# The second MLP product of nine blocks by seven half-size products in place of eight, with its sums formed on chip

## The chip, the cores and the metric

The kernel runs on one core of one Trainium2 chip. Times are device microseconds (us). Most executions of one kernel agree within some tenths of a per cent; others fall into a slower state, some per cent longer, mostly at a granted TensorE clock below 1. PE is the engine that multiplies, ACT the one for activations and evictions, DVE the vector engine, POOL the GpSimd engine, SP the one that issues transfers. SBUF is the on-chip memory, and a PSUM bank is where a product accumulates.

## The reference

```python
# q, k, v: 4 batches x 8 heads x 768 positions x 64;  4 sinks, window of 128
scores = scale * q @ k.T                    # kept: the first 4 positions and the last 128
a = softmax(where(keep, scores, -1e9))
x = (a @ v)  -> 3072 tokens x 512
h = x @ w_in                                # 512 x 2048
g = h / (1 + exp(-1.702 * h))
out = g @ w_out                             # 2048 x 512
```

Of PE's work the MLP is much the larger part, and it goes block by block: 12 blocks of 256 tokens, each with attention, a first product (64 matmuls of 256 columns) and a second one (32 matmuls of 512 columns).

## The kernel before

The kernel is not written in its final order. Every piece of work is declared with its inputs, a priority and an assumed duration for each engine that may do it. A scheduler then plays all of that through on paper and emits one fixed program for each engine, in the order that it arrived at. In the traces below each engine works off its list in order, and an instruction whose inputs are there waits behind the ones before it: in the changed kernel (e1_again below) DVE starts block 2's first sum at 54.3 us, and POOL's first sum, of the same inputs, starts at 68.13 us, behind weight sums and casts.

```python
class Plan:
    def op(self, eng, dur, lat, fn, deps=(), prio=0.0, acq=None, rel=(), kind=""):
        return self.any({eng: (dur, lat)}, lambda _: fn(), deps, prio, acq, rel, kind)
    ...
        def could(o, e):
            ...
            s = max([free[e], o.begin] + [after(d, e) for d in o.deps])
```

The activation of a block (`gT`, 2048 features x 256 tokens in fp16) comes in eight pieces from DVE, each a tanh from ACT combined with the bank of the first product. The second product takes it as weights:

```python
    def mm2(k):
        ...
        for j, c0, c1 in ((0, 0, 512), (1, 0, 512)) if k < NK - 1 else (...):      # j: half of the tokens
            for s in range(NS):                                                   # NS = 8
                def f(...):
                    for Fi in (2 * s, 2 * s + 1):
                        nc.tensor.matmul(
                            f32(holder[0])[:, 0:w], g[:, Fi, bass.ts(j, P)], w_out16[:, Fi, c0:c1],
                            start=(Fi == 0), stop=(Fi == NF - 1),
                        )
                ...
            # then one eviction by ACT (times 0.5) and two transfers out
```

The softmax here doesn't subtract the row's maximum and nothing guards it: scores larger than these inputs give would overflow.

## Time and profile before

The 222.08 us (median of three; 221.85 to 227.37) divide as follows. Shares are of the profiled execution's span of 220.0 us.

| engine | busy us | share | what it does in the steady part |
|---|---|---|---|
| PE | 213.7 | 97% | both MLP products, scores, attention |
| DVE | 125.9 | 57% | activation pieces, masks, normalising |
| ACT | 125.7 | 57% | tanh, exponentials, evictions |
| POOL | 87.0 | 40% | casts of q, k, v, up to 157 us |

The prediction below shows the page's own lines. The table by stage: for a stretch of time, each engine's busy us with its instruction count in brackets, then granted clock, share of the transfer engines, and GB/s.

```profile
core 0: us, PE busy (x) PEld busy (x) DVE busy (x) ACT busy (x) POOL busy (x), PEclk, DMA share, GB/s
47.00:64.00 17.00, 17.00 (x174) 11.83 (x169) 12.34 (x31) 10.18 (x21) 15.00 (x27) 1.00 0.98 227
64.00:81.00 17.00, 17.00 (x197) 11.84 (x196) 10.50 (x23) 11.75 (x23) 9.27 (x15) 1.00 0.83 195
```

PE is full in both. POOL is nearly full in the first and half free in the second.

### The profile page before, as it was taken

The page shows a single profiled execution, that of the slowest core. Times are in us where ns is not written, and L with a number is a line of the kernel's source. Part 1 is how long each engine was busy: PE and PEld are TensorE (multiplying, and loading weights), DVE is VectorE, ACT ScalarE, POOL GpSimd, SP SyncE. Part 2 cuts the span into 40 slices and gives each one's busy share as a digit, 9 for nine tenths or more (in the row PEclk, how much of TensorE's full clock was granted, in tenths as well). Part 3 has the DMA queues.
Part 4 walks back from the last instruction along what each step waited for, and adds up shares of the span by engine and source line. Part 5 has one row for each costly group of instructions (what it writes and reads, how often), then busy time and mean ns, then how long its engine had stood idle before and what let it go on. Part 6 is the DMA issues. An engine that isn't in the chain of part 4 may idle for free.

```text
span 220.0 us, 5209 instructions
## 1 busy us (share of the span) xinstructions
PE 213.7 (97%) x2066; PEld 143.8 (65%) x2066; DVE 125.9 (57%) x274; ACT 125.7 (57%) x243; POOL 87.0 (40%) x150
## 2 busy tenths in 40 slices
PE   7889999999999999999999999999999999999993
PEld 3448777577757766666666667657667666666642
DVE  2678855397826855656556664666465655634310
ACT  2597645777557576475485476466466486444320
POOL 2596431689971956704905727508500000000000
PEclk9999999999999999999999999999999999999998
DMA  5999999999979589289498589398541312231223
GB/s 162 355 236 204 207 302 202 324 302 289 210 141 240 143 182 295 51 166 297 103 205 240 73 204 250 84 213 232 106 91 47 71 27 48 52 68 26 51 48 95
DMA packets 65911, 36.54 MB, mean 166 GB/s; under 512 B 27968, under 2 KB 61120, under 8 KB 65888
## 3 DMA queue, kind: packets, MB, share of 16 engines
q1 hardware_dynamic: 60848, 30.19, 56.0%
q0 software_dynamic: 4592, 5.37, 12.9%
q10 hardware_dynamic: 448, 0.66, 1.1%
q8 instruction: 16, 0.26, 0.5%
q14 instruction: 7, 0.06, 0.1%
HBM read 27.56 MB, written 6.29 MB: 154 GB/s over the span
## 4 chain that ended last, share of the span: by engine, by line
PE 91%; DMA 4%; ACT 2%; SPq 1%; issue 0%; DVE 0%
PE bank L736 39%; PE bank L765 37%; PE bank L669 6%; PE bank L604 5%; DMA qk<-in_q_dram 3%; PE bank L532 1%; DMA out_dram<-osb 1%; ACT at L629 1%; ACT v L286 1%; PE bank L596 1%; PE bank L584 1%; PE bank L708 1%; SPq L407 0%; PE bank L846 0%; ACT blkT L286 0%
## 5 line engine op out<-in xcount | busy, mean ns | idle before, releaser
L765 PE MATMUL bank<-w_out,gT 128*128 128x512 f16 (+2 forms) x400 | 99.8, 371 | 0.0
L736 PE MATMUL bank<-xT,w_in 128*128 128x256 f16 x768 | 99.8, 273 | 0.0
L750 DVE SCALAR_TENSOR_TENSOR gT<-th,bank 128x512 f16<-128x512 f16 x96 | 65.5, 683 | 48.8 <-ACT th L748 47.8
L748 ACT ACTIVATE th<-bank 128x512 f16<-128x512 f32 x96 | 57.7, 603 | 62.0 <-PE bank L736 61.3
L736 PEld LDWEIGHTS <-w_in 128*128 128x128 f16 x768 | 72.9, 98 | 23.8 <-issue 1.7
L286 POOL CAST qk<-qk 64x512 f16<-64x512 f32 (+1 forms) x74 | 44.9, 609 | 45.1 <-DMA qk<-in_q_dram 41.9
L629 ACT ACTIVATE at<-bank 128x512 f16<-128x512 f32 (+1 forms) x96 | 48.7, 569 | 10.9 <-PE bank L604 10.9
L765 PEld LDWEIGHTS <-gT 128*128 128x128 f16 x400 | 36.1, 98 | 23.3 <-issue 1.4
L636 DVE TENSOR_TENSOR at<-at,bank 128x1024 f16<-128x1024 f16 (+1 forms) x40 | 25.7, 643 | 22.8 <-ACT at L629 22.8
L286 POOL CAST v<-v 64x512 f16<-64x512 f32 (+1 forms) x43 | 26.1, 606 | 8.9 <-DMA v<-in_v_dram 6.8
L669 PE MATMUL bank<-v,at 128*128 128x65 f16 x352 | 21.2, 193 | 0.1
L784 ACT ACTIVATE osb<-bank 128x512 f32<-128x512 f32 (+1 forms) x24 | 14.4, 600 | 11.0 <-PE bank L765 11.0
L669 PEld LDWEIGHTS <-at 128*128 128x128 f16 x352 | 17.5, 97 | 4.2 <-DVE at L636 0.3
L689 DVE TENSOR_TENSOR xb<-bank,rcp 128x256 f16<-128x256 f32 x36 | 15.2, 422 | 0.7
L669 PE MATMUL bank<-vs,ats 128*128 128x65 f16 x128 | 14.7, 193 | 0.0
L604 PEld LDWEIGHTS <-blkT 64*128 64x128 f16 x256 | 8.0, 94 | 9.3 <-issue 7.8
L604 PE MATMUL bank<-blkT 64*128 64x256 f16 x192 | 13.4, 244 | 0.0
L669 PEld LDWEIGHTS <-ats 128*128 128x128 f16 x128 | 12.0, 97 | 2.0
L687 DVE RECIPROCAL rcp<-bank 128x4 f32<-128x4 f32 x48 | 8.4, 177 | 3.6 <-PE bank L669 3.2
L286 ACT COPY blkT<-bank 128x256 f16<-128x256 f16 (+1 forms) x12 | 5.1, 463 | 4.4 <-PE bank L532 4.3
L604 PE MATMUL bank<-blkT,blkT 64*128 64x128 f16 x64 | 7.2, 222 | 0.0
L846 PE MATMUL bank<-zero 128*128 128x512 f16 x19 | 5.8, 463 | 1.2 <-DVE zero L304 1.2
(43 smaller groups left out, 68.4 us busy)
## 6 DMA issues: line engine op xcount, KB each, us to landing
v<-in_v_dram SPq DMA_DIRECT2D x12, 512.0 KB, 6.7
out_dram<-osb SPq DMA_DIRECT2D x46, 128.0 KB, 2.4
qk<-in_q_dram SPq DMA_DIRECT2D x8, 512.0 KB, 5.3
qk<-in_k_dram SPq DMA_DIRECT2D x8, 512.0 KB, 6.7
w_in<-in_moe_w_in_dram POOLq DMA_DIRECT2D x4, 512.0 KB, 9.5
w_out<-in_moe_w_out_dram POOLq DMA_DIRECT2D x4, 512.0 KB, 12.8
qk<-in_q_dram SPq DMA_DIRECT2D x6, 256.0 KB, 5.3
qk<-in_k_dram SPq DMA_DIRECT2D x4, 256.0 KB, 5.5
```

Source lines behind the costliest of these rows:

```text
L286: {"POOL": nc.gpsimd.tensor_copy, "DVE": nc.vector.tensor_copy, "ACT": nc.scalar.copy}[e](out=out, in_=in_)
L604: nc.tensor.matmul(f32(o_s, 2 * n + i)[:, c : c + w], src[d, j], Q[d].rearrange("d j s -> d (j s)")[:, q0 : q0 + w], start=k >= KM, stop=T ...
L629: nc.scalar.activation(out=A[:, i, 0:W], in_=f32(o_s, 2 * n + i)[:, 0:W], func=AF.Exp, scale=scale)
L636: nc.vector.tensor_tensor(out=A[:, :, 0:W], in0=A[:, :, 0:W], in1=mask(c0, c0 + W).unsqueeze(1).to_broadcast((P, 2, W)), op=ALU.mult,)
L669: nc.tensor.matmul(avp()[:, j, i], a_, v_, start=(n == 0), stop=(n == len(mms) - 1))
L687: o_r = op("DVE", 93, 190, lambda: nc.vector.reciprocal(out=rc, in_=avp()[:, :, :, D]), [o_a], prio=base - 1.2 * h8, kind="rcp")
L689: o_n = op("DVE", 340, 430, lambda: nc.vector.tensor_tensor(out=X, in0=avp()[:, :, :, 0:D], in1=rc.to_broadcast((P, 2, 2, D)), op=ALU.mult ...
L736: nc.tensor.matmul(f32(holder[0])[:, bass.ts(e, TB)], w_in16[:, c, bass.ts(Fi, P)], X[:, c] if k < KX else X2[:, :, c], start=(c == 0), st ...
L748: o_t = op("ACT", 477, 600, lambda first=first: nc.scalar.activation(out=th[first.places[0]], in_=f32(first), func=AF.Tanh, scale=0.851), ...
L750: o_g[k, s] = op("DVE", 590, 700, lambda first=first, s=s: nc.vector.scalar_tensor_tensor(out=g[:, 2 * s : 2 * s + 2].rearrange("p a t -> ...
L765: nc.tensor.matmul(f32(holder[0])[:, 0:w], g[:, Fi, bass.ts(j, P)], w_out16[:, Fi, c0:c1], start=(Fi == 0), stop=(Fi == NF - 1),)
L784: nc.scalar.mul(O[:, c0:c1], f32(holder[0])[:, 0:w], 0.5)
```

## The change

Strassen's scheme multiplies two 2x2 matrices of blocks with seven block products instead of eight, at the price of sums of blocks on both inputs and of the results. Here the blocks are halves of the tokens and of the feature pairs on the one side, halves of the features and of the output columns on the other. PE loses an eighth of the second product's columns in blocks 2 to 10; POOL and DVE get the sums. The core of the diff:

```diff
-    RS, RQ, RV, RA, RX, RG, RTH, RO = 3, 2, 4, 6, 3, 5, 3, 3
+    RS, RQ, RV, RA, RX, RG, RTH, RO = 3, 2, 4, 4, 3, globals().get('OPT',{}).get('RG',3), 3, 2
+    KS, LASTS = globals().get('OPT',{}).get('KS',2), globals().get('OPT',{}).get('LASTS',NK-1)
...   # the third input buffer is a tile "third", whose room three of the weight sums take over later
+    def forms_of_w():                       # once: 4 x 5 sums of 128 x 512 fp16
+        for j in range(4):
+            for n, (a, b_, what) in enumerate((((0, 0), (1, 1), ALU.add), ...)):
+                def f(eng, j=j, n=n, a=a, b_=b_, what=what):
+                    x = slice(2 * j, 2 * j + 2)
+                    (nc.gpsimd if eng == "POOL" else nc.vector).tensor_tensor(
+                        out=wf[n][:, x], in0=W[:, x, a[0], a[1]], in1=W[:, x, b_[0], b_[1]], op=what)
+                ...
+                o_wf[j, n] = plan.any({"POOL": (OPT_("WFP", 800), OPT_("WFP", 800) + 100), **({"DVE": (350, 450)} if OPT_("WFD", 0) else {})}, ...)
+    def forms_of_g(k):                      # each block: 4 x (DVE sum, DVE difference, POOL sum)
+        for s in range(0, NS, 2):
+            def f1(x=x):
+                nc.vector.tensor_tensor(out=F[:, x, 0:2], in0=G[:, x, 0:2], in1=G[:, x, 2:4], op=ALU.add)
+            def f2(x=x):
+                nc.vector.tensor_tensor(out=G[:, x, 1:3], in0=G[:, x, 1:3], in1=G[:, x, 0::3], op=ALU.subtract)
+            def f3(eng, x=x):
+                (nc.gpsimd if eng == "POOL" else nc.vector).tensor_tensor(
+                    out=F[:, x, 2], in0=G[:, x, 0], in1=G[:, x, 3], op=ALU.add)
+    def mm2_by_seven(k):                    # 56 matmuls of 256 columns, in three banks
+        last = run(2, lambda s: [(0, G[:, s, 0], wf[1][:, s]), (1, G[:, s, 3], wf[2][:, s])], hu, ...)
+        ...   # ACT: lone = .5 half;  DVE: lone += .5 other half
+        last = run(4, lambda s: [(0, F[:, s, 2], wf[0][:, s])], hy, ...)
+        ...   # DVE: lone += .5 of it
+        last = run(2, lambda s: [(0, F[:, s, 0], W[:, s, 1, 1]), (1, F[:, s, 1], W[:, s, 0, 0])], hu, ...)
+        ...   # ACT evicts two quarters; POOL: part = lone - them (fp32)
+        last = run(2, lambda s: [(0, G[:, s, 2], wf[4][:, s]), (1, G[:, s, 1], wf[3][:, s])], hw, ...)
+        ...   # DVE: the other two quarters = .5 of the bank + part; four transfers out
+    def second(k):
+        if KS <= k < LASTS:
+            mm2_by_seven(k)
+        else:
+            mm2(k)
```

In the views, `third` and `wf` are the weight sums, `gF` and the second writing of `gT` the activation sums, and L863 the new matmuls.

More of the change, by code (lines that the diff above doesn't have):

```diff
@@ L253 @@
     vs32 = pool.tile([P, B, E], FP32, name="vs32")
-    qk32 = ring("qk32", RS, (P, 2, H, 2, D), FP32)
-    v32 = ring("v32", RS, (P, H, 2, D), FP32)
+    third = pool.tile([P, 3 * H * 2 * D], FP32, name="third")
+    qk32 = ring("qk32", RS - 1, (P, 2, H, 2, D), FP32)
+    v32 = ring("v32", RS - 1, (P, H, 2, D), FP32)
+    qk32.append(third[:, 0 : 2 * H * 2 * D].rearrange("p (e h i d) -> p e h i d", e=2, h=H, i=2))
+    v32.append(third[:, 2 * H * 2 * D :].rearrange("p (h i d) -> p h i d", h=H, i=2))
+    wf = [third[:, 1024 * n : 1024 * n + 1024].bitcast(FP16).rearrange("p (s c) -> p s c", s=NS) for n in range(3)]
+    wf += ring("wf", 2, (P, NS, d_model // 2), FP16)
+    gF = ring("gF", 2, (P, NS, 3, P), FP16)
+    part = pool.tile([P, 512], FP32, name="part")
+    lone = pool.tile([P, 256], FP32, name="lone")
     qk16 = ring("qk16", RQ, (P, 2, 2, H, D), FP16)
@@ L265 @@
     gT = ring("gT", RG, (P, NF, TB), FP16)
-    osb = ring("osb", RO, (P, d_model), FP32)
+    osb = ring("osb", RO, (P, 2 * d_model), FP32)
     bank = [psp.tile([P, 512], FP32, name=f"bank{i}") for i in range(8)]
-    plan = Plan(8, {"m": 1, "s": 5, "t": 4, "a": 2, "x": 2, "h": RTH, "o": 2})
+    OPT_ = globals().get("OPT", {}).get
+    plan = Plan(8, {"m": 1, "s": 5, "t": 4, "a": 2, "x": 2, "h": RTH, "o": OPT_("NO", 3)})
     op = plan.op
@@ L394, in load @@
         b, r = divmod(k, R)
-        sl = k % RS
+        sl = k if k < RS else (k - 1) % (RS - 1)
         t0 = r * TB
@@ L719 @@
     o_g = {}
-    n_o = [0]
     def mm1(k):
@@ L775, in mm2 @@
             if not c0:
-                oi = n_o[0] % RO
-                n_o[0] += 1
-                war = reuse("osb", oi)
-            O = osb[oi]
+                war = reuse("osb", (k % RO, j))
+            O = osb[k % RO][:, bass.ts(j, d_model)]
             row = k * TB + j * P
@@ L798, in mm2 @@
                 o_d = op(eng, 590, (420, 4), f, o_c, prio=prio, kind="out")
-                uses("osb", oi, o_d)
+                uses("osb", (k % RO, j), o_d)
+    def forms_of_w():
+        W = w_out16.rearrange("p (s e) (h c) -> p s e h c", e=2, h=2)
+        for j in range(4):
+            for n, (a, b_, what) in enumerate((((0, 0), (1, 1), ALU.add), ((0, 1), (1, 1), ALU.subtract), ((1, 0), (0, 0), ALU.subtract),
+                                    ((0, 0), (0, 1), ALU.add), ((1, 0), (1, 1), ALU.add))):
+                def f(eng, j=j, n=n, a=a, b_=b_, what=what):
+                    x = slice(2 * j, 2 * j + 2)
+                    (nc.gpsimd if eng == "POOL" else nc.vector).tensor_tensor(
+                        out=wf[n][:, x], in0=W[:, x, a[0], a[1]], in1=W[:, x, b_[0], b_[1]], op=what)
+                free = []
+                if n < 3:
+                    free = [o for (kk, _, _), o in o_cqk.items() if kk == 2] + [o for p in range(NP) for o in o_cv[2, p]]
+                o_wf[j, n] = plan.any({"POOL": (OPT_("WFP", 800), OPT_("WFP", 800) + 100), **({"DVE": (350, 450)} if OPT_("WFD", 0) else {})},
+                                      f, [o_w[4 + j]] + free, prio=nominal(KS + 1, -9 + j), kind="wf")
@@ new lines, in forms_of_g @@
+    def forms_of_g(k):
+        g, F = gT[k % RG], gF[k % 2]
+        G = g.rearrange("p (s e) (t q) -> p s (e t) q", e=2, t=2)
+        war = reuse("gF", k % 2)
+        for s in range(0, NS, 2):
+            x = slice(s, s + 2)
+            def f1(x=x):
[5 more added lines that the diff above has]
+                    out=F[:, x, 2], in0=G[:, x, 0], in1=G[:, x, 3], op=ALU.add)
+            prio = nominal(k, s + OPT_("GF", 3)) + 3
+            deps = [o_g[k, s], o_g[k, s + 1]]
+            a = op("DVE", 335, 440, f1, deps + war, prio=prio, kind="gf")
+            b_ = op("DVE", 335, 440, f2, deps + [a], prio=prio, kind="gf")
+            e3 = OPT_("F3", "POOL").split()
+            c = plan.any({e: {"POOL": (450, 550), "DVE": (200, 300)}[e] for e in e3}, f3, deps + war, prio=prio, kind="gf")
+            for i in (s, s + 1):
+                o_f[k, i] = (a, b_, c)
@@ new lines, in mm2_by_seven, with run, f, at @@
+    def mm2_by_seven(k):
+        g, F, O, T = gT[k % RG], gF[k % 2], osb[k % RO], part
+        G = g.rearrange("p (s e) (t q) -> p s (e t) q", e=2, t=2)
+        W = w_out16.rearrange("p (s e) (h c) -> p s e h c", e=2, h=2)
+        N = d_model // 2
+        u = [0]
+        def run(n_s, what, first, deps, fresh, acq=None):
+            prev = None
+            holder = first
+            for s0 in range(0, NS, n_s):
+                def f(s0=s0):
+                    for s in range(s0, s0 + n_s):
+                        for half, lhs, rhs in what(s):
+                            nc.tensor.matmul(f32(holder[0])[:, bass.ts(half, N)], lhs, rhs, start=fresh and s == 0 and half == 0,
+                                             stop=s == NS - 1, skip_group_check=True)
+                n = n_s * len(what(0))
+                o = op("PE", n * pe_ns(N), (n - 1) * pe_ns(N) + N / 2.4 + 166, f,
+                       deps(range(s0, s0 + n_s)) + ([prev] if prev else []), prio=at(),
+                       acq=None if holder else acq, kind="mm2")
+                u[0] += 1
+                if not holder:
+                    holder.append(o)
+                uses("gT", k % RG, o)
+                uses("gF", k % 2, o)
+                prev = o
+            return prev
+        def at():
+            return nominal(k + 1, 8 * u[0] / 14) + 3
+        def fw(n, S):
+            return [o_wf[s // 2, n] for s in S]
+        hu, hy, hw = [], [], []
+        last = run(2, lambda s: [(0, G[:, s, 0], wf[1][:, s]), (1, G[:, s, 3], wf[2][:, s])], hu,
+                   lambda S: [o_g[k, s] for s in S] + fw(1, S) + fw(2, S), True, ("o", 1))
+        o_x = op("ACT", 263, 390, lambda: nc.scalar.mul(lone, f32(hu[0])[:, 0:N], 0.5), [last] + reuse("lone", 0), prio=at(), kind="y")
+        o_y = op("DVE", 335, 440, lambda: nc.vector.scalar_tensor_tensor(
+            out=lone, in0=f32(hu[0])[:, N : 2 * N], scalar=0.5, in1=lone, op0=ALU.mult, op1=ALU.add), [o_x], prio=at(), kind="y")
+        last = run(4, lambda s: [(0, F[:, s, 2], wf[0][:, s])], hy,
+                   lambda S: [o_f[k, s][2] for s in S] + fw(0, S), True, ("o", 1))
+        o_z = op("DVE", 335, 440, lambda: nc.vector.scalar_tensor_tensor(
+            out=lone, in0=f32(hy[0])[:, 0:N], scalar=0.5, in1=lone, op0=ALU.mult, op1=ALU.add), [last, o_y], prio=at(), rel=[(hy[0], 0)], kind="y")
+        last = run(2, lambda s: [(0, F[:, s, 0], W[:, s, 1, 1]), (1, F[:, s, 1], W[:, s, 0, 0])], hu,
+                   lambda S: [o_x, o_y] + [o_f[k, s][0] for s in S], False)
+        war = reuse("osb", (k % RO, 0)) + reuse("osb", (k % RO, 1))
+        o_u = op("ACT", 477, 600, lambda: nc.scalar.mul(O[:, N : 3 * N], f32(hu[0]), 0.5), [last] + war,
+                 prio=at(), rel=[(hu[0], 0)], kind="oc")
+        o_t = plan.any({e: {"POOL": (1100, 1200), "DVE": (600, 700)}[e] for e in OPT_("TE", "POOL").split()},
+            lambda eng: (nc.gpsimd if eng == "POOL" else nc.vector).tensor_tensor(
+            out=T.rearrange("p (n c) -> p n c", n=2), in0=lone.unsqueeze(1).to_broadcast((P, 2, N)),
+            in1=O[:, N : 3 * N].rearrange("p (n c) -> p n c", n=2), op=ALU.subtract),
+            [o_z, o_u] + reuse("part", 0), prio=at(), kind="t")
+        uses("lone", 0, o_t)
+        last = run(2, lambda s: [(0, G[:, s, 2], wf[4][:, s]), (1, G[:, s, 1], wf[3][:, s])], hw,
+                   lambda S: [o_f[k, s][1] for s in S] + fw(3, S) + fw(4, S), True, ("o", 1))
+        o_v = op("DVE", 600, 700, lambda: nc.vector.scalar_tensor_tensor(
+            out=O.rearrange("p (n c) -> p n c", n=4)[:, 0::3], in0=f32(hw[0]).rearrange("p (n c) -> p n c", n=2), scalar=0.5,
+            in1=T.rearrange("p (n c) -> p n c", n=2), op0=ALU.mult, op1=ALU.add),
+            [last, o_t], prio=nominal(k + 1, 8) + 3, rel=[(hw[0], 0)], kind="oc")
+        uses("part", 0, o_v)
+        for j in range(2):
+            row = k * TB + j * P
+            for i in range(2):
+                def f(i=i, j=j, row=row):
+                    nc.sync.dma_start(
+                        out[row : row + P].rearrange("(p i) f -> i p f", i=2)[i], O[64 * i : 64 * i + 64, bass.ts(j, d_model)])
+                o_d = op("SP", 590, (420, 4), f, [o_v, o_u], prio=nominal(k + 1, 8) + 4, kind="out")
+                uses("osb", (k % RO, j), o_d)
@@ L801 @@
+    o_wf, o_f = {}, {}
+    def second(k):
[3 more added lines that the diff above has]
+            mm2(k)
     for j_ in range(8):
@@ L811 @@
             mm1(k_ - 1)
+            if KS <= k_ - 1 < LASTS:
+                forms_of_g(k_ - 1)
+        if k_ == 2:
+            forms_of_w()
         if k_ >= 2:
-            mm2(k_ - 2)
+            second(k_ - 2)
     mm1(NK - 1)
-    mm2(NK - 2)
-    mm2(NK - 1)
+    if LASTS == NK:
+        forms_of_g(NK - 1)
+    second(NK - 2)
+    second(NK - 1)
     loads += o_vl + [o_more]
```

## The prediction

> **What bounds the kernel now.** I read the page's part 1 first, then the slices, the chain that ended last, the groups by form, and last the timeline. Part 1 and three rows of the slices:
>
> ```profile
> span 220.0 us, 5209 instructions
> PE 213.7 (97%) x2066; PEld 143.8 (65%) x2066; DVE 125.9 (57%) x274; ACT 125.7 (57%) x243; POOL 87.0 (40%) x150
> ...
> PE   7889999999999999999999999999999999999993
> DVE  2678855397826855656556664666465655634310
> POOL 2596431689971956704905727508500000000000
> PEclk9999999999999999999999999999999999999998
> ```
>
> PE is at 9 from slice 4 to the last but one, at full clock; DVE and ACT are near half. POOL matters though it shows 40%: it has nothing after slice 31 and is at 9 in slices 9 to 10, 13 and 19. Is the busy PE really streaming? The chain, merged in time, shows the spacing (start, us, what):
>
> ```profile
> PE 91%; DMA 4%; ACT 2%; SPq 1%; issue 0%; DVE 0%
> ...
> 206.12 0.87 PE bank L736 x8
> 208.73 4.33 PE bank L765 x20
> 214.22 2.37 DMA out_dram<-osb
> ```
>
> Eight 256-column products (first MLP product) take 0.87 us, 109 ns each; twenty 512-column ones (second) 4.33 us, 216 ns each: a column costs the same in either shape. From 20 us on the table by stage gives PE 10.00 of 10.00 and 17.00 of 17.00 in each stretch up to 200 us, so a column taken away there shortens the time, if the rest keeps up. The list of waits has PE waiting three times, 2.6 us in all, before 15 us. The bound is the number of columns through PE.
>
> The groups that I size with (busy us, mean ns | idle before):
>
> ```profile
> L736 PEld LDWEIGHTS <-w_in 128*128 128x128 f16 x768 | 72.9, 98 | 23.8 <-issue 1.7
> L750 DVE SCALAR_TENSOR_TENSOR gT<-th,bank 128x512 f16<-128x512 f16 x96 | 65.5, 683 | 48.8 <-ACT th L748 47.8
> L636 DVE TENSOR_TENSOR at<-at,bank 128x1024 f16<-128x1024 f16 x28 | 19.2, 685 | 16.9 <-ACT at L629 16.9
> L689 DVE TENSOR_TENSOR xb<-bank,rcp 128x256 f16<-128x256 f32 x36 | 15.2, 422 | 0.7
> L479 POOL TENSOR_TENSOR vs<-vs,more 128x520 f16<-128x520 f32 x4 | 4.2, 1054 | 0.3
> L784 ACT ACTIVATE osb<-bank 128x512 f32<-128x512 f32 x23 | 13.9, 604 | 9.0 <-PE bank L765 9.0
> ```
>
> [...] The mask product (L636) agrees: 546 ns at 768 elements and 685 at 1024 is 0.54 ns an element. [...] No DVE instruction of the steady part before has two SBUF inputs (each one's second input is PSUM)[...]; the change adds eight per block. [...] L479 gives 1054/520 = 2.0 ns, on fp32 inputs; no 16-bit two-input sum on POOL is in the trace.
>
> **The change part by part.**
>
> *PE.* A block's second product is 2 x 16 matmuls of 512 columns: 32 x 215.8 ns = 6.91 us. By seven products it is 7 x 8 of 256 columns: 56 x 109.2 = 6.12 us. Saved 0.79 us a block, times 9 blocks: **7.1 us**. I counted the built programs too: 400 matmuls become 112 + 504, and the sum of PE's work at these spacings falls from 204.0 to 196.8 us, nothing else altered. There are 216 more weight loads of 98 ns, but the first MLP product loads 128 columns of weights per 256-column matmul already and still runs at 109, so they stay hidden.
>
> *ACT.* Two evictions of 604 ns become one of 604 and one of 128x256 (388 by the L616 group of that form): 0.2 us a block less. Nothing.
>
> *DVE, per block.* Four sums and four differences of 512 fp16 elements, 685 - 512 x 0.54 = 407 ns each: 3.26 us; two combinations of 256 out of PSUM, 422 each (form of L689): 0.84; one of 512, 683: 0.68. Together 4.8 us recorded, some 4 net, since consecutive DVE records overlap by about 0.09 (99.12 to 99.71 us for a 0.66 record). A 17 us stretch holds 9.4 to 12.3 us now; a block of about 16 us would then hold 13 to 14.5: **some 85%**. It still fits.
>
> *POOL, per block.* Twelve casts at 0.65 spacing (8 in 5.29 us): 7.8; four sums of 256, at 2 ns about 0.55: 2.2; one fp32 of 512: 1.05. That is 11 of 16 us, fine in the long run.
>
> *POOL, once.* Twenty weight sums of 512, between 0.8 us (what the kernel's scheduler assumes) and 1.05 (L479): 16 to 21 us, all before block 2's second product. This is where I expect loss. Before, POOL between 40 and 65 us is packed:
>
> ```profile
> 40.39 2.62 POOL L286 CAST v<-v 64x512 f16<-64x512 f32 x4 [6.79 <-DMA v<-in_v_dram]
> 43.07 2.28 POOL L286 CAST qk<-qk 128x512 f16<-128x512 f32 x4
> 45.30 2.61 POOL L286 CAST v<-v 64x512 f16<-64x512 f32 x4
> ...
> 49.10 5.29 POOL L286 CAST qk<-qk 64x512 f16<-64x512 f32 x8
> 54.45 2.59 POOL L286 CAST v<-v 64x512 f16<-64x512 f32 x4
> 57.11 5.18 POOL L286 CAST qk<-qk 64x512 f16<-64x512 f32 x8
> ```
>
> In the new order eight weight sums lie ahead of the casts of block 2's v, in the idle time there; twelve come after 43 us. I add up in the built order, with the shorter and the longer size: casts of block 4's q and k end at 60.9 (62.9) instead of 54.4; of block 5's at 72.6 (75.5) instead of 62.3; the last of block 2's POOL sums at 73.0 (76.0). PE's program places the first scores of block 4 at 62.2 us of its work, the last use of that sum at 62.7, the first scores of block 5 at 69.4. Before, time runs 8.2 us ahead of that work (64.24 us at 56.07 of work). Casts to landed transpose is 6.5 us (tile blkT's landing). So block 4's scores are safe (67.4 or 69.4 against 70.4 plus), the last sum is late by 1.5 us (about 4.5), and block 5's scores then lose little more. [...] I take **2.2 us**. Four weight sums also come before block 2's q and k casts at 31.07; these then end about 2 us later, while PE's transposes of them were moved back 0.9 us: **0.6 us**.
>
> *Steady part.* [...] The bank of a first-product group has room (three in turn, a group every 2 us, tanh plus product 1.3), so most is hidden; I take **0.1 us a block, 0.9 us**.
>
> *Rings and end.* gT 5 to 3, input buffers 3 to 2, at 6 to 4 copies: each still allows about a block of lead. The last block stays in the old form, so the end (PE alone, then 2.4 us of output) stays.
>
> Sum: 222.1 - 7.1 + 2.2 + 0.6 + 0.9 = **218.7 us**; I set 218.4, as orders like this one are usually shaped until they run well.
>
> **Rivals.** *A: PE takes it all.* For: PE waits for nothing now, the other engines average 57% and less. Then 215 us. *B: DVE becomes the bound* [...] With 0.6 us a block lost: 221 us or more. *C: POOL in one stage only* (my choice): the loss comes once, between 60 and 85 us, and later blocks run at 0.79 us less each. *D: weight loads bound the 256-column matmuls*, the gain vanishes at 222; against it stands L736 at 109 ns.
>
> **Range and chances.** A gives the low end, 215.2; B with C the high end, 222.0. Faster by 2% needs under 217.6, which is stage losses of 2.7 us or less in place of my 3.7: 0.40. Within 2%: 0.55. Slower by 2%, over 226.5, needs DVE or POOL as a full bound: 0.05.
>
> **What would show it.** PE: 504 matmuls of 128x256 in the new line at 109 ns spacing, PE work down by 7 us; another spacing is D. POOL: weight sums between 0.8 and 1.05 us; slices 6 to 13 at 9; PE's list of waits with POOL sums or a transposed qk as releasers near 70 to 80 us, 1.5 to 4.5 us in all. Port: the DVE sums over 407 ns in the mean, above all where POOL is busy, near 407 after its casts end. Stretches of 17 us after 100 us with PE full prove A or C there; PE idle in each of them proves B. I am wrong if PE is full throughout (faster than said), or if DVE is at 9 in most slices (slower).

The sum came to 222.1 - 7.1 + 2.2 + 0.6 + 0.9 = 218.7 us and was set to 218.4. The 0.9 us (steady part), a share of the 2.2 us (POOL, once) and rival B rested on a passage by which DVE and POOL hold each other up, the author's estimate, not shown at the time ("Port" in its last paragraph is the name for it). 109.2 ns is the mean of 491 spacings of L736 in the trace of the kernel before, and 215.8 ns that of its longest run of L765 at 512 columns (14 matmuls; all 217 spacings average 216.2 ns). The mask product's 0.54 ns an element is measured, with one input in PSUM.

## More of the kernel before

The casts of q, k and v from fp32 to fp16 fall mostly to POOL, in time that nothing else wants:

```python
        ns = {"POOL": (n / 0.96 + 30, n / 0.96 + 130), "DVE": (n / 1.92 + 65, n / 1.92 + 165),
              ...
```

## The result, and the profile after

The changed kernel is correct and took 225.77 us (median of four, 225.32 to 230.92), against 222.15 for the kernel before beside it (median of four, 221.85 to 227.37). The ratio is 1.016, with a 95% interval of 1.013 to 1.020. Ratios here are the mean time of one kernel's fast runs over that of the other's fast runs of the same rounds, so they are not quite the ratio of the medians. By the 2% rule that counts as the same; it is surely not faster, and it lies above the predicted range.

The first profile of the changed kernel fell into the slow state (clock 0.985), so the lines below are from its repetition `e1_again`, at full clock, 225.42 us. The page, parts 1 and 2:

```profile
span 223.6 us, 5862 instructions
...
PE 209.5 (94%) x2282; PEld 164.8 (74%) x2282; DVE 176.4 (79%) x372; ACT 123.1 (55%) x244; POOL 152.1 (68%) x215
...
PE   7989999999794689999999999999999999999993
...
POOL 2596498899999999999659998599696232131200
```

A digit is 5.6 us. PE has a dent in the eleventh (56 to 61 us) and a hole from the thirteenth to the fifteenth (67 to 84 us), and looks full elsewhere. POOL stands at 8 or 9 from the sixth to the nineteenth (28 to 106 us). The chain that ended last, by engine, was 91% PE before; now a quarter of it is POOL:

```profile
PE 45%; POOL 26%; DVE 16%; issue 4%; ACT 4%; DMA 3%; SPq 1%; DVEq 0%; POOLq 0%; ACTq 0%
```

The same two stretches as before, by stage:

```profile
47.00:64.00 17.00, 15.84 (x165) 11.17 (x162) 15.76 (x36) 9.46 (x20) 16.39 (x21) 1.00 0.67 185
64.00:81.00 17.00, 11.20 (x131) 8.83 (x130) 11.20 (x17) 7.25 (x15) 16.20 (x24) 1.00 0.33 66
```

PE now idles 1.16 and 5.80 us of these, 7.0 us in all; POOL is full in both. From 81 to 183 us PE idles another 1.7 us. Outside these stretches its idle time is what it was, less 0.8 us at the start. The list of PE's waits (what it waited for: us in total, times, longest) names POOL first and DVE second, and the timeline of PE shows the two long ones (start, us, what, and in brackets the idle time before it):

```profile
PE bank L863 <- POOL gF L836: 5.0, 2, 2.6
PE bank L679 <- DVE at L646: 2.1, 4, 1.2
```

```profile
72.26 0.39 PE L863 MATMUL bank<-third,gF 128*128 128x256 f16 x2 [2.46 <-POOL gF L836]
...
78.95 0.39 PE L863 MATMUL bank<-third,gF 128*128 128x256 f16 x2 [2.58 <-POOL gF L836]
```

These are block 2's second product, waiting for activation sums on POOL. The timeline of POOL says what it was doing instead:

```profile
49.53 9.31 POOL L816 TENSOR_TENSOR third<-w_out 128x512 f16<-128x512 f16 x8
58.77 5.57 POOL L296 CAST qk<-qk 64x512 f16<-64x512 f32 x8
64.43 3.74 POOL L816 TENSOR_TENSOR third<-w_out 128x512 f16<-128x512 f16 x3
...
72.78 5.37 POOL L296 CAST qk<-qk 64x512 f16<-64x512 f32 x8
78.23 1.29 POOL L836 TENSOR_TENSOR gF<-gT 128x256 f16<-128x256 f16 x2
```

Weight sums, casts, sums, casts, in the order that the scheduler had fixed. Of the block's four sums the second and third stand behind the casts of v (from 68.74 us) and start at 71.48 us; the fourth stands behind eight casts of q and k. The fourth ends near 78.9 us, the first of the last line's two.

The DVE wait is a second mechanism. Timeline of DVE, then of PE, from the same execution:

```profile
55.45 1.26 DVE L834 TENSOR_TENSOR gT<-gT 128x512 f16<-128x512 f16 x1
56.63 0.54 DVE L646 TENSOR_TENSOR at<-at,bank 128x768 f16<-128x768 f16 x1
```

```profile
57.23 0.35 PE L679 MATMUL bank<-v,at 128*128 128x65 f16 x6 [1.16 <-DVE at L646]
```

The DVE difference of 512 elements, sized at 0.41 us, took 1.26 us, while POOL was in its run of weight sums of 1.16 us each; the mask product queued behind it, and PE waited 1.16 us for that. The groups by form (busy us, mean ns | idle before) show that this is the rule and not one case:

```profile
L836 POOL TENSOR_TENSOR gF<-gT 128x256 f16<-128x256 f16 x36 | 26.4, 734 | 27.0 <-DVE gT L759 24.2 <-PE bank L614 1.8
L834 DVE TENSOR_TENSOR gT<-gT 128x512 f16<-128x512 f16 x36 | 24.9, 693 | 0.8
...
L832 DVE TENSOR_TENSOR gF<-gT 128x512 f16<-128x512 f16 x36 | 23.1, 640 | 0.7
...
L816 POOL TENSOR_TENSOR third<-w_out 128x512 f16<-128x512 f16 x12 | 14.2, 1214 | 0.2
```

The DVE differences average 693 ns and the DVE sums (L832) 640 ns. The timeline also shows what they take alone: the two at 187.68 and 188.13 us overlap no POOL instruction and took 0.41 and 0.42 us. In the first profile seven of the 72 overlap none, and these took 408 to 425 ns, against means of 660 and 705 ns. So two inputs in SBUF are not slow in themselves. The eight weight sums of the other group (`wf`) took 1153 ns each.

So there are two suspects: the twenty weight sums on POOL before block 2 (called W), and DVE and POOL holding each other up (called P). The texts, the labels and the code call P "the port". That is a name here: the runs show how much the two engines' instructions lengthen beside each other, and not what they share.

### The profile page after: what moved, and what is told of

It is laid out like the page before. It is cut to its first block, busy times and chain, and to the rows that moved or that the text cites. A ratio compares the mean times of both kernels' runs of the same rounds, so it can differ in the third digit from the quotient of the medians.

```text
span 229.1 us, 5862 instructions
## 1 busy us (share of the span) xinstructions
PE 211.8 (92%) x2282; PEld 166.2 (73%) x2282; DVE 178.0 (78%) x372; ACT 123.3 (54%) x244; POOL 151.5 (66%) x215
## 4 chain that ended last, share of the span: by engine, by line
PE 51%; POOL 20%; DVE 12%; issue 3%; DMA 2%; ACT 1%; DVEq 0%; POOLq 0%; ACTq 0%
PE bank L745 22%; PE bank L863 13%; POOL qk L296 8%; PE bank L774 7%; POOL third L816 6%; PE bank L679 5%; DVE gT L759 4%; POOL gF L836 2%; POOL v L296 2%; PE bank L614 2%; DVE gT L834 2%; DMA xT<-xb 2%; DVE at L646 2%; DVE gF L832 1%; POOL part L899 1%
## 5 line engine op out<-in xcount | busy, mean ns | idle before, releaser
L836 POOL TENSOR_TENSOR gF<-gT 128x256 f16<-128x256 f16 x36 | 26.6, 740 | 27.6 <-DVE gT L759 26.0
L863 PEld LDWEIGHTS <-gT 128*128 128x128 f16 x288 | 27.1, 98 | 5.5 <-DVE gT L759 1.4
L834 DVE TENSOR_TENSOR gT<-gT 128x512 f16<-128x512 f16 x36 | 25.4, 705 | 0.8
L863 PEld LDWEIGHTS <-gF 128*128 128x128 f16 x216 | 20.1, 98 | 7.9 <-POOL gF L836 5.6
L832 DVE TENSOR_TENSOR gF<-gT 128x512 f16<-128x512 f16 x36 | 23.8, 660 | 0.7
L774 PE MATMUL bank<-w_out,gT 128*128 128x512 f16 (+2 forms) x112 | 23.9, 349 | 0.0
L863 PE MATMUL bank<-w_out,gF 128*128 128x256 f16 x144 | 21.0, 273 | 0.0
L899 POOL TENSOR_TENSOR part<-lone,osb 128x512 f32<-128x512 f32 x9 | 11.5, 1280 | 13.0 <-ACT osb L896 12.7
L863 PE MATMUL bank<-wf,gT 128*128 128x256 f16 x144 | 20.0, 273 | 0.0
L863 PE MATMUL bank<-third,gT 128*128 128x256 f16 x144 | 19.0, 273 | 0.9 <-POOL third L816 0.8
```

Source lines behind the costliest of these rows:

```text
L774: nc.tensor.matmul(f32(holder[0])[:, 0:w], g[:, Fi, bass.ts(j, P)], w_out16[:, Fi, c0:c1], start=(Fi == 0), stop=(Fi == NF - 1),)
L832: nc.vector.tensor_tensor(out=F[:, x, 0:2], in0=G[:, x, 0:2], in1=G[:, x, 2:4], op=ALU.add)
L834: nc.vector.tensor_tensor(out=G[:, x, 1:3], in0=G[:, x, 1:3], in1=G[:, x, 0::3], op=ALU.subtract)
L836: (nc.gpsimd if eng == "POOL" else nc.vector).tensor_tensor(out=F[:, x, 2], in0=G[:, x, 0], in1=G[:, x, 3], op=ALU.add)
L863: nc.tensor.matmul(f32(holder[0])[:, bass.ts(half, N)], lhs, rhs, start=fresh and s == 0 and half == 0, stop=s == NS - 1, skip_group_check ...
```

## The experiments

Each was built from the changed kernel. Before is the kernel before in the same job, with fast runs of 221.3 to 222.4 us wherever a ratio is given. "Wrong" means that the output is not right and only the time counts. A few of the fast runs had a granted clock of about 0.99 (226.10 of e1_again, 223.37 of e12); with the runs nearer full clock alone, e1_again would be 1.016 and e12 0.996, which changes no reading below.

| run | what it is | fast runs, us | ratio to before (95%) |
|---|---|---|---|
| e1_again | the change as it is | 225.42, 226.10 | 1.018 (1.014 to 1.021) |
| e2_noport | DVE sums read PSUM for one input; wrong | 222.00, 222.43 | 1.002 (0.999 to 1.005) |
| e3_nowsum | weight sums of 4 columns; wrong | 218.95, 220.42 | 0.990 (0.985 to 0.996) |
| e4_neither | both | 216.81 to 218.87 | 0.981 (0.975 to 0.986) |
| e5_rings | the smaller buffer rings alone, old product | 221.48 to 221.88 | 1.000 (0.998 to 1.001) |
| e6_late4 | seven products from block 4 on | 218.51 to 219.30 | 0.987 (0.984 to 0.989) |
| e7_late4_known | the same, better informed scheduler | 216.16 to 217.39 | 0.976 (0.973 to 0.979) |
| e8_late3_dve | from block 3 on, weight sums on DVE or POOL, informed | 215.24 to 216.87 | 0.973 (0.970 to 0.977) |
| e12_sizes_again | e6 with measured durations only | 220.32 to 223.37 | 1.000 (0.992 to 1.008) |
| e13_noport_again | e6 with DVE sums reading PSUM; wrong | 215.96 to 216.88 | 0.976 (0.973 to 0.978) |
| e14_neither_again | e4, ordered with measured durations; wrong | 214.68 to 215.94 | 0.971 (0.968 to 0.975) |
| e15_late3_again | e8's kernel again | 215.29 to 216.47 | 0.973 (0.970 to 0.977) |

### The change again, and each suspect taken away (one job)

**e1_again** is the changed kernel unchanged, for a clean profile and a reference on this chip.

> The changed kernel itself once more, for a profile in the fast state (the first fell in the slow one) and as the yardstick of the other three. All theories: about 225.5 us, ratio to before 1.015. PE should wait some 5 to 8 us between 45 and 100 us, on POOL's weight sums and on the block-2 activation sums of POOL, as in the first profile.

It came as before, 1.018.

**e2_noport** takes P away without altering any order or dependency: the second input of each DVE activation sum becomes a constant that lies in PSUM.

```diff
-                nc.vector.tensor_tensor(out=F[:, x, 0:2], in0=G[:, x, 0:2], in1=G[:, x, 2:4], op=ALU.add)
+                nc.vector.tensor_tensor(out=F[:, x, 0:2], in0=G[:, x, 0:2], in1=mask(0, 512).rearrange("p (a b c) -> p a b c", a=2, b=2), op=ALU.add)
...   # f2 likewise
```

> Wrong result on purpose. The order of all engines is kept; the eight DVE sums of a block take their second input from a PSUM tile (the mask) in place of SBUF, 16-bit and of the same size. Theory P[...]: DVE sums fall from about 680 ns to about 410, POOL weight sums and casts shorten too where a DVE sum had blocked them, time falls by 2 to 4 us to about 222. Theory W (POOL's own weight sums in one stage are the loss[...]): time falls by under 1.5 us. Rival S (the sums are slow by their shape[...]): they stay near 680 ns and the time stays.

```profile
L836 POOL TENSOR_TENSOR gF<-gT 128x256 f16<-128x256 f16 x36 | 24.0, 669 | 28.7 <-DVE gT L759 22.3 <-PE bank L614 4.6 <-DVE rcp L697 0.8
...
L834 DVE TENSOR_TENSOR gT<-gT,bank 128x512 f16<-128x512 f16 x36 | 15.0, 416 | 0.8
```

The same instruction, in the same place of the same program, went from 693 to 416 ns; L832 from 640 to 415. POOL gained too: its sums from 734 to 669 ns, its casts of q and k from 664 to 609, so the blocking goes both ways. Rival S of the expectation, slow by shape, falls. The time fell by 1.018 - 1.002, 1.6% or 3.5 us of 221.8, and the two intervals do not touch. PE became full from 47 to 64 us, but from 64 to 81 us it still idled 5.2 us: P is real and does not explain the hole.

**e3_nowsum** takes W away in the same manner: each weight sum keeps its place and its dependencies but handles 4 columns in all.

```diff
-                        out=wf[n][:, x], in0=W[:, x, a[0], a[1]], in1=W[:, x, b_[0], b_[1]], op=what)
+                        out=wf[n][:, x, 0:2], in0=W[:, x, a[0], a[1], 0:2], in1=W[:, x, b_[0], b_[1], 0:2], op=what)
...   # the matmuls read quarters of w_out in place of the sums: same shapes, same count
```

> Wrong result on purpose. Order kept; each of the twenty weight sums on POOL is cut to 2 columns of its 256 and the matmuls read quarters of the weight itself in their place, so no matmul waits for a weight sum and POOL is some 20 us freer between 28 and 75 us. Theory W: PE's idle time between 45 and 100 us goes from 6 or 7 us to under 2 and the time falls by 5 us or more, to 220 or less. Theory P: it falls by 2 to 3 us, the rest of the loss is spread over all blocks.

PE's waits for POOL are gone from its list, and the stretch of the hole reads:

```profile
64.00:81.00 17.00, 16.07 (x203) 13.30 (x201) 14.59 (x30) 9.74 (x20) 11.91 (x17) 1.00 0.67 154
```

PE idles 0.93 us there instead of 5.80. The time fell by 1.018 - 0.990, 2.7% or 6.1 us. W is the larger cause.

**e4_neither** does both edits.

> Wrong result on purpose: both edits of the two runs before it. If port and weight sums are the whole loss, PE keeps its saving of 7 us and the time is 215 to 216 us. If rings, DVE's plain load or the order cost something as well, it stays above 217.

The ratio is 0.981, 8.2 us below the change. The two single effects add up to 9.6 us. An overlap is plausible, as some of P's blocking happens behind weight sums: in e3 the DVE sums fell to 617 and 651 ns. But 1.4 us is no more than the intervals allow. Fully hidden sums would have left 0.968 (7.1 us below 221.8), so about 2.8 us were still unaccounted for.

### Buffers, and a later start (another job)

**e5_rings** keeps the old product everywhere and takes over only the smaller rings and the shared tile.

```diff
+OPT = {'KS': 12}
...
-        if k_ == 2:
-            forms_of_w()
```

> Correct result. The changed kernel with no block by seven products and no weight sums: what is left of the change is its smaller buffers (two input buffers after block 2, three gT, four at, two double-width osb). Theory R (the smaller rings cost time): 223 us or more. Theories W and P: as before, 222 us within 0.5.

1.000 within 0.2%: with the old product the smaller buffers cost nothing. With the new one they were not varied; e14 below, which keeps them, leaves about 0.7 us for them and all else.

**e6_late4** asks whether W is a matter of when. One number moves the start of the new product from block 2 to block 4, which gives up two of the nine savings (1.6 us). All twenty weight sums remain, of full size, on POOL.

```diff
+OPT = {'KS': 4}
```

> Correct result, one number changed: seven products in blocks 4 to 10 in place of 2 to 10, which lets the scheduler put the weight sums some 35 us later. The saving on PE is 7 x 0.79 = 5.5 us in place of 7.1. Theory W: the stage loss of about 6 us goes almost wholly, the port's loss stays: 222.0 - 5.5 + 2 to 3 = 219 us. If the weight sums hurt wherever they stand: 222 us or more.

0.987, and correct. The stretch of the hole, and POOL in it:

```profile
64.00:81.00 17.00, 17.00 (x197) 11.76 (x196) 10.36 (x23) 11.55 (x23) 16.54 (x20) 1.00 0.71 171
```

```profile
66.11 11.17 POOL L817 TENSOR_TENSOR third<-w_out 128x512 f16<-128x512 f16 x10
```

POOL now does ten weight sums in a row at 66.11 us, 11.17 us long, in a stretch where before it was half free, and PE is full, 17.00 of 17.00, in each of the three stretches from 47 to 98 us. The sums take 1152 ns each, as before: their cost is their deadline and not their amount. What remains is 1.56 us of PE idle time from 115 to 132 us, behind DVE.

**e7_late4_known** tells the scheduler what the traces showed: POOL's durations as measured, and a rule that keeps DVE's two-input sums and POOL's work apart, since they lengthen beside each other (640 and 693 ns in e1_again, 415 and 416 in e2).

```diff
+        port = [0.0]
+        def on_port(o, e):
+            return o.kind in (("cqk", "cv", "ks", "vs", "gf", "wf", "t") if e == "POOL" else ("gf", "wf")) and e in ("POOL", "DVE")
...
+            if on_port(o, e):
+                s = max(s, port[0])
...
+            if on_port(o, e):
+                port[0] = s + dur - 20
...   # POOL: cast n / 0.96 + 30 -> + 117;  weight sum 800 -> 1165;  activation sum 450 -> 675;  fp32 sum 1100 -> 1280
```

> Correct result. As the run before it, but the kernel's scheduler is given the measured durations (POOL weight sum 1.165 us for 0.8, POOL activation sum 0.675 for 0.45, fp32 sum 1.28 for 1.1, cast 0.65 for 0.56) and keeps two-input DVE sums and POOL work from overlapping. No instruction is added or removed. If the rest of the loss is an order made for wrong sizes and a port it did not know, this is faster than the run before it by 1 to 2 us: 217 to 218 us. If the port's waits themselves bind DVE, it is not.

0.976: another 1.0% off, with no arithmetic altered. The DVE sums (L832 and L834's counterparts) fell from 728 and 628 ns in e6 to 572 and 474; the first of the two, in e6 and then in e7:

```profile
L833 DVE TENSOR_TENSOR gF<-gT 128x512 f16<-128x512 f16 x28 | 20.4, 728 | 0.6
...
L841 DVE TENSOR_TENSOR gF<-gT 128x512 f16<-128x512 f16 x28 | 15.9, 572 | 0.3
```

**e8_late3_dve** starts one block earlier and lets the scheduler place weight sums on DVE.

```diff
+OPT = {'KS': 3, 'WFD': 1}
...   # and the scheduler of e7
```

> Correct result. The informed scheduler, seven products in blocks 3 to 10, and weight sums on either DVE or POOL as the scheduler finds room. Saving on PE 8 x 0.79 = 6.3 us; with little loss 216 to 217 us, the best so far, and faster than the kernel before by over 2%. If DVE, near 85% busy, can't take the eight or more microseconds of weight sums too, 219 us or more.

It put 18 of the 20 weight sums on DVE, at 504 ns and 649 ns in its two groups, and two on POOL at 1149 and 1154 ns. The ratio is 0.973, with a correct result: a version that beats both kernels, by 2.7% and, across the two jobs, some 4.4%. The stretch of the hole:

```profile
64.00:81.00 17.00, 17.00 (x176) 11.44 (x174) 15.80 (x33) 10.05 (x20) 9.88 (x15) 1.00 0.71 172
```

Against e7 its interval overlaps; one more block should be worth 0.36%, and 0.3% is what shows, but these runs do not prove it.

### A job without a usable reference

Three more kernels ran next, to split e7's two pieces of knowledge and to find the rest of e4's gap.

> Wrong result on purpose: nine blocks, DVE sums off the port, weight sums cut to 2 columns (as the fourth run of the first set), but the order made with the measured POOL durations. In the fourth run 2.3 us of the 7.1 were still missing. If those came from an order laid out for too short POOL work: ratio 0.968 to 0.972, 215 us. If from DVE's plain load: 0.98 as there.

> Correct result. Blocks 4 to 10, the scheduler knows the measured durations but nothing of the port. It tells the two parts of the informed scheduler apart: if sizes alone are enough, 0.976 as with both; if it is the port rule, 0.987 as with neither.

> Wrong result on purpose. Blocks 4 to 10 in the order of the plain scheduler, DVE sums with one operand in PSUM. Theory P: the 1.3% by which that order fell short of the informed one is waits at the port, so this gives 0.975 to 0.978; if the rest is the order itself, 0.983 or more.

On that chip the kernel before fell into the slow state in six of its seven runs, so no ratio could be formed. The fast times alone (e9 215.88 and 216.91, e10 222.24 and 224.06, e11 216.17 to 217.63) point where the repetitions then went.

### The same three again, and the best one

**e12_sizes_again** is e7 without its rule against overlap: only the durations in the scheduler are altered.

> The kernel of run e10 again, because the kernel before fell into the slow state there in six runs of seven and no ratio came of it. From e10's fast runs (222.2 and 224.1 us): the durations alone do not help and may hurt, ratio 0.99 to 1.01; the port rule carries the informed scheduler's gain.

1.000, not better than e6 but worse by 1.3% (0.9% with the runs nearer full clock alone). Its DVE sums took 755 and 687 ns. So the durations alone do not make e7 good; the rule is needed. Whether the rule alone would do was not run. Why better durations gave a worse order is only argued: the scheduler, which knows nothing of P, happened to pack more DVE sums against POOL's work.

**e13_noport_again** is e6, order and all, with e2's edit.

> The kernel of run e11 again, for a ratio; wrong result on purpose. 0.975 to 0.979: most of what the plain order lost against the informed one in blocks 4 to 10 is waits at the port.

0.976 against e6's 0.987: in blocks 4 to 10, P alone cost 1.1%, 2.4 us in seven blocks, 0.35 us a block. And e7, which obeys the rule against overlap with right results, stands at the same 0.976: the order wins back what P took. Both stand 5.3 to 5.4 us below the kernel before, of the 7 x 0.79 = 5.5 us that PE saves. So with a later start and P out of the way nearly the whole saving arrives, with all weight sums at full size, and in e13 even in an order made for the wrong durations.

**e14_neither_again** is e4 with the nine blocks, ordered with durations as they are measured (and 205 ns for the shrunk weight sums).

> The kernel of run e9 again, for a ratio; wrong result on purpose. 0.968 to 0.973: with the port, the weight sums and the mis-sized order all taken away, nearly the whole saving of 7.1 us (3.2%) is there.

0.971: 2.1 us less than e4, so most of e4's remaining gap seems to be its order, made for POOL instructions that do not last what it assumed (the jobs differ, and the intervals touch at 0.975). Among these are the shrunk weight sums themselves, planned at 800 ns and lasting 204, so the 2.1 us belong to e4 and are not shown for the change. PE waits for no POOL instruction in it. That is 6.4 of the 7.1 us that fewer columns promised; the last 0.7 us stay open.

**e15_late3_again** is e8's kernel once more.

> The best kernel again on another chip, beside the runs before it. Correct result; 0.970 to 0.977 as before.

0.973 again, on the same chip as e8 (chip 8), and not on another as the expectation has it. One of its four executions, the profiled one, took 1199.52 us, at clock 1.0: PE counted busy 1193 us (208 us in e8) for the same 2258 matmuls, with all slices alike. The records of its 256-column products average 1028 to 1051 ns in place of 273, those of its weight loads (gT, gF) 310 and 322 ns in place of 98, while DVE was busy no longer than in e8 (171.6 and 171.8 us): only PE and its weight loads were slow (POOL's sums took 696 and 710 ns, ACT's tanh 597 and 604), and the recorded clock does not show it. It did not come again in the other seven runs of this kernel, it is left out as an outlier, and I have no explanation.

## Why the prediction was wrong

- **PE's saving was right.** "Saved 0.79 us a block, times 9 blocks: 7.1 us". The 504 matmuls run at 109 ns spacing in the trace, and e14, with nothing else in the way, gained 6.4 us. Rival D falls: the additional weight loads, 98 ns each, stay hidden. In the changed kernel PE's busy time fell by only 4.2 us (213.7 to 209.5), which was not explained by a run (a guess from two numbers: a record lasts 273 ns at a spacing of 109, so a short wait need not show as idle); the idle time rose by 7.8 us (6.3 to 14.1). 7.8 plus the missing 2.9 is 10.7 us of losses, where I had 3.7.
- **The step that failed most is "POOL, once".** "I take 2.2 us" for a place that I had named correctly, down to block 2's last POOL sum and eight casts. Idle time from 47 to 81 us was 7.0 us, and e3 puts the weight sums' effect at 6.1 us. The terms of the sum were too small: weight sums took 1.15 to 1.21 us, not "0.8 to 1.05", so 23.2 us of POOL and not 16 to 21; POOL's activation sums took 0.67 us in e2 and 0.73 in e1_again on average, not 0.55. The last sum was to be done at 73.0 (76.0) us; it was done near 78.9. I had a sum with two ends, 1.5 and 4.5 us, and chose near the lower one, though the only two-input POOL sum in the trace pointed to the upper. Of the two long waits I also foresaw only the one for the last sum; the one for the second sum, behind the casts of v, cost as much (2.46 and 2.58 us).
- **The 0.6 us for late q and k casts did not come.** From 20 to 47 us PE is full, 27.00 of 27.00, and the transposed q and k appear in its waits with 0.3 us in all.
- **"Steady part", 0.1 us a block, 0.9 us, was mis-sized four times over.** I expected DVE to be held up by POOL, an estimate that no trace showed then, and hid almost all of it behind three banks in turn. The sums lengthened by 225 to 277 ns in the mean (e2 against e1), 2.0 us in a block's eight. What was wrong is the hiding: DVE serves PE in order, so a mask product behind a blocked sum makes PE wait at once, as at 57.23 us (1.16 us); such waits come to 2.1 us in the changed kernel and are gone from PE's list in e2. It cost 3.5 us (e2); in the steady blocks alone 0.35 us each (e13 against e6). Rival B was nearer: "With 0.6 us a block lost: 221 us or more". DVE was also nearly full. From 47 to 183 us, the hole left out, it was busy 15.8 of 17 us a stretch, in two of them 16.7; in e2, without P, 14.7. So "some 85%" was right for the work (87%), and P made it 93%. The sign that I gave for being wrong, DVE at 9 in most slices, came in half of them (20 of 40), and in 16 of the 19 from slice 18 to 36.
- **The last move had no ground.** "I set 218.4, as orders like this one are usually shaped until they run well" moved the number the wrong way. This order had been shaped by durations that POOL does not keep, and by a scheduler that does not know P.
- **Rings and end** were right as far as tested: e5 gives 1.000 with the old product, and the end is as before.
- **The class was luck.** I gave "within 2%" the best chance, and the ratio of 1.016 is in it, but on the slow side, which I had not argued for.
- **Slips in the working**, none of which decided the number. 12.3 us in a stretch plus 4 for the sums makes 15.6 us in a block of 16, not 14.5. POOL's slices are counted from zero and PE's from one, and POOL has nothing after slice 29, not 31. The mask product (L636) has one input in PSUM, so it showed nothing for two inputs in SBUF (measured later, alone: 408 to 425 ns for 512 elements).

In one line, from what the runs show: 222.1 - 7.1 + about 6 (weight sums with a deadline) + about 3.5 (P), less about 1.4 (both taken away together), + about 2.1 (e4's order) + 0.7 (open), comes to about 226. These terms are differences of runs, so they must add up; the first two losses are the ones shown for the change itself.

## What to carry to other kernels

Work taken from the bound engine is a gain only if the helpers' added work has no deadline where they are full: sum up the helper's queue up to the first consumer at the rate of the trace's slowest similar instruction, and if it comes out late, start the new scheme later; here one number gave back more than it cost. Treat two engines that lengthen each other's instructions as one resource in a schedule: in this kernel (DVE's sums 640 and 693 ns in place of 415, POOL's casts 664 in place of 609) their collisions hurt through what stood behind them in order, 3.5 us in all. Give an order-making scheduler the collision rule along with the measured durations: here the durations alone did not help, and the rule alone was not tried.

## What the runs show of single instructions

- A DVE sum of 512 fp16 elements with both inputs in SBUF averaged 640 to 693 ns beside a POOL that was 68% busy (e1_again) and 415 ns with one input in PSUM (e2); POOL's casts went from 664 to 609 ns by the same edit. In this kernel that was worth 3.5 us of 225, through in-order queues, at a DVE that was 79% busy over the span.
- On POOL, a two-input sum of 512 fp16 elements took 1.15 us (e2), 2.25 ns an element, and one of 256 took 0.67 us. The fp32 sum of 512 in the same kernel (one of its inputs read twice over) took 1.27 us, and the one of 520 from fp32 to fp16 1.06 us; as an estimate, the two fp16 sizes give about 0.19 us fixed and 1.9 ns an element.
- On DVE, 512 fp16 elements took 415 ns with one 16-bit input in PSUM (e2), and 408 to 425 ns with both in SBUF where no POOL instruction overlapped (first profile of the changed kernel): no difference by the place of the input alone.
- One execution of e15 took 1199.52 us at a recorded full clock, with PE busy 1193 us in place of e8's 208.
